# Infini-attention with a mixer MLP, in float32 from pairs: phi read from PSUM, casts and an update on other engines, and a head pipeline of three stages in another order

## The chip, the cores and the metric

The kernel runs on one core of a Trainium2 chip. The metric is the device time of one execution in microseconds (us), median of several runs. The engines are TensorE (PE; its weight loads are shown apart as PEld), VectorE (DVE), ScalarE (ACT), GpSimd (POOL) and SyncE (SP), which here only issues transfers.

## What is computed

2048 tokens of width 1024 pass a pre-norm block: attention with a compressive memory, then an MLP. There are 32 heads of width 32, and 4 segments of 512 tokens.

```python
phi = lambda t: jnp.where(t > 0, t + 1.0, jnp.exp(t))
g = _sigmoid(beta).reshape(1, H, 1, 1)
for s in range(N):
    qs, ks, vs = q[:, :, s], k[:, :, s], v[:, :, s]
    logits = jnp.einsum("bhqd,bhkd->bhqk", qs, ks) * scale + mask
    a_dot = jnp.einsum("bhqk,bhkd->bhqd", _softmax(logits), vs)
    pq = phi(qs)
    num = jnp.einsum("bhld,bhde->bhle", pq, M)
    den = jnp.einsum("bhld,bhd->bhl", pq, z)[..., None] + 1e-6
    outs.append(g * num / den + (1.0 - g) * a_dot)
    pk = phi(ks)
    M = M + jnp.einsum("bhld,bhle->bhde", pk, vs)
    z = z + jnp.einsum("bhld->bhd", pk)
...
h = x + attention(layernorm(x))
h2 = h + (gelu(layernorm(layernorm(h)) @ w1 + b1) @ w2 + b2)
```

The inner softmax is causal within a segment; M and z carry what earlier segments held.

## The kernel before

Float32 products are made of three products of a faster format: each operand is split into a high part (a cast) and a low part (the operand less its high part), and `mm3` (L110) adds high x high, high x low and low x high in PSUM. So every operand costs a cast and a subtraction, and the kernel spreads these over VectorE, ScalarE and GpSimd: for weights `split` (L87) and `load_block` (L193, wh is the high part, wl the low one).

The 2048 tokens go in two halves of two segments each. `attention(half)` (L201) walks over 8 groups g of 4 heads, and for each over its two segments sl. One group in one segment is a *unit* here, so there are 16 units in a half, and a pair of units shares the weights of its group. For a unit, `dense` (L268) makes kps, qps and vps, the transposed projections of 128 x 512, each of 8 steps c of three products (24 steps in all), and `heads` (L482) does the softmax attention of the *previous* unit, one head in each of 4 slots. A slot has 6 steps, written out in `PLAN` (L30), and `interleave` (L509) takes one step of `heads` after each step of `dense`. The order of the program is the order in which each engine gets its instructions, and an engine takes them strictly in that order.

A letter in `PLAN` is one operation of a head, its digit a part of it:

- `q`: scores of one block of queries (TensorE L396 into bank pqk), then VectorE adds the mask and finds the minimum (L397), then ScalarE takes the exponential (L405).
- `n`: VectorE takes reciprocals of the sums (L409), GpSimd scales the rows by them and by 1 - sigmoid(beta) (L412).
- `t`: TensorE transposes the probabilities into bank ppt (L428, group 0, 1 or 2), ScalarE casts them to pth (L430).
- `s`, `S`: VectorE subtracts for ptl (L435).
- `a`: TensorE multiplies with the values (L448, po), ScalarE copies one half of po to ot (L453).
- `o`: VectorE adds the other half (L459); after the fourth head GpSimd adds the memory's part omt (L462), and SP stores it.

Small letters are of the current head or the one before (p1), `S`, `a` and `o` of the one before that (p2): two heads stand in the pipe.

Within `dense`, the projections give more work. kh and qh are casts (ScalarE L277, L291), kl and ql subtractions (VectorE L283, L298); 24 transfers on SP rearrange them per head into ks and qs. phi(k) and phi(q) are min(exp(x), 1) + max(x, 0): ScalarE writes both terms from PSUM (L229, L230), VectorE adds them (L235). pk is transposed (pkn). MZ holds M and z of all groups; its high part mzh is a VectorE cast (L310). `late` (L330) is the rest of a unit and runs in steps during the next unit: vn (values transposed back), the memory's products pm and their division (VectorE L344 to L347 into om), the products pmm of the memory's update (VectorE adds them to M, L362, and the sum of pk to z, L363), and om transposed (pom) and copied (ScalarE L378, omt). The products of pm and pmm are small; they lie in a list, and `one_small` (L249) places one of them ahead of a transposition or a product of `a`.

PSUM has 8 banks: three shared by kps, qps, vps, pkn, vn, pm, pmm and pom, two for pqk, two for ppt, one for po. Temporaries in SBUF come from `tmp` (5 slots) and `tmpr` (6 slots).

The weights of the next group are loaded and split at the end of a pair (`weights`, L490): wh by VectorE (L89), only in the first group's wq and wv by ScalarE (L91); wl by GpSimd (L92). At the start of a half `ln1` (L181) loads x and normalizes it (GpSimd makes the scale factor v, L123 and L124, VectorE or ScalarE applies it); behind attention come the output projection `wo_seg` (L536), the second norm and the MLP, which are not touched.

Of the kernel before, what the change touches and what calls it, by code (L numbers as in the profile page):

```python
# [42 lines left out]
def build(tc, x, wq, wk, wv, wo, beta, w1, b1, w2, b2, out):  # L43
# [157 lines left out]
    def attention(half):  # L201
# [16 lines left out]
        def tmpr(name):  # L218
            return ab.tile([P, 512], F32R, tag="tmpr", name=name, bufs=6)

# [5 lines left out]

        def phi_parts(ps):
            e, r = tmp("e"), tmp("r")
            nc.scalar.activation(e, ps, AF.Exp)  # L229
            nc.scalar.activation(r, ps, AF.Relu)  # L230
            return e, r

        def phi_sum(parts, name, acc=None):
            o = tmp(name)
            nc.vector.scalar_tensor_tensor(o, parts[0], 1.0, parts[1], op0=ALU.min, op1=ALU.add, accum_out=acc)  # L235
            return o
# [11 lines left out]

        def one_small():  # L249
            if small:  # L250
                small.pop(0)()
# [16 lines left out]
        def dense(g, sl, ws, u):  # L268
# [9 lines left out]
            if s < 3:  # L278
                kparts = phi_parts(kps)
            qps = ps_dense("qps")  # L280
            for c in project(ws["q"], sl, "qps", qps):
                if c == 0:
                    nc.vector.tensor_tensor(kl, kps, raw(kh), op=ALU.subtract)  # L283
                    u["ks"] = stack(kh, kl, "ks", (0, 1, 0))
                if c == 2 and s < 3:
                    zc = ab.tile([P, 64], F32, name="zc", bufs=2)[:, 0:1]
                    pk = phi_sum(kparts, "pk", zc)
                next(behind, None)
                yield
            qh, ql = tmpr("qh"), tmpr("ql")  # L290
            nc.scalar.copy(qh, qps)  # L291
            if s > 0:
                qparts = phi_parts(qps)

            vps = ps_dense("vps")
            for c in project(ws["v"], sl, "vps", vps):
                if c == 0:
                    nc.vector.tensor_tensor(ql, qps, raw(qh), op=ALU.subtract)  # L298
                    u["qs"] = stack(qh, ql, "qs", (0, 0, 1))
                if s > 0:  # L300
                    if c == 2:
                        pq = phi_sum(qparts, "pq")
                    if c == 4:
                        while small:
                            one_small()
                        pqh, pql = tmpr("pqh"), tmpr("pql")
                        mzh = ab.tile([P, 256], F32R, name="mzh", bufs=1)[:, 0:132]
                        mzl = ab.tile([P, 256], F32R, name="mzl", bufs=1)[:, 0:132]
                        nc.scalar.copy(pqh, pq)
                        nc.vector.tensor_copy(mzh, MZ[:, g, :])  # L310
                        nc.gpsimd.tensor_tensor(mzl, MZ[:, g, :], raw(mzh), op=ALU.subtract)
                    if c == 5:
                        nc.gpsimd.tensor_tensor(pql, pq, raw(pqh), op=ALU.subtract)
                if c == 1 and s < 3:
                    pkn = ps_dense("pkn")
                    for i in range(4):
                        nc.tensor.transpose(pkn[:, i * P:(i + 1) * P], pk[:, i * P:(i + 1) * P], ident)
# [8 lines left out]
            vs = ab.tile([P, 16, 64], F32R, name="vs", bufs=2)  # L326
            u["vs"] = vs
            omt = u["omt"] = tmp("omt") if s > 0 else None

            def late():  # L330
# [3 lines left out]
                vn3 = vn.rearrange("p (a b) -> p a b", b=DH)  # L334
                nc.scalar.copy(vs[:, :, 0:32], vn3)
                nc.vector.tensor_tensor(vs[:, :, 32:64], vn3, raw(vs[:, :, 0:32]), op=ALU.subtract)
                yield
                if s > 0:
                    om = tmp("om")

                    def memory(i2, ps):
# [3 lines left out]
                        nc.vector.reciprocal(rg, rg)  # L345
                        nc.vector.tensor_tensor(rg, rg, gate[:, 0:1, 4 * g:4 * g + 4].to_broadcast([P, 2, 4]), op=ALU.mult)
                        nc.vector.tensor_tensor(  # L347
# [10 lines left out]
                if s < 3:  # L358
                    def update(pmm):
                        for j in range(4):  # L360
                            b = slice(32 * j, 32 * j + 32)
                            nc.vector.tensor_tensor(MZ[b, g, b], pmm[b, b], MZ[b, g, b], op=ALU.add)  # L362
                        nc.vector.scalar_tensor_tensor(MZ[:, g, 128:132], hsel, zc, MZ[:, g, 128:132], op0=ALU.mult, op1=ALU.add)  # L363

# [5 lines left out]
                while len(small) > total - left:  # L370
                    yield
                yield
                if s > 0:
                    pom = ps_dense("pom")
                    for i in range(4):
                        one_small()
                        nc.tensor.transpose(pom[:, i * P:(i + 1) * P], om[:, i * P:(i + 1) * P], ident)
                    nc.scalar.copy(omt, pom)  # L378
                while small:
# [35 lines left out]
        def ptr(st, n):  # L415
# [21 lines left out]
        def av(st, n):  # L437
# [4 lines left out]
            for jk in (0, 1) if n == 0 else (3, 2):  # L442
                w = 512 - P * jk
                v = u["vs"][:, 4 * jk + j, :]
                for part in ("pth", "ptl"):
                    if (jk, part) != (3, "ptl"):
                        one_small()
                    nc.tensor.matmul(po[:, P * jk:], v, st[part][:, koff[jk]:koff[jk] + w],  # L448
                                     start=(jk, part) == (0, "pth"), stop=(jk, part) == (2, "ptl"))
# [14 lines left out]

        pipe = [None, None]

        def slot(cur):
            p1, p2 = pipe
# [11 lines left out]
            pipe[0], pipe[1] = cur, p1  # L480

# [697 lines left out]
```

## Time and profile before

| | |
|---|---|
| median of 3 runs | 2394.48 us (2393.11 to 2403.72) |
| the profiled execution | 2394.96 us, its span 2393.2 us |
| granted TensorE clock | 0.993 |
| busy: PE, DVE, ACT, POOL | 2308.3, 1628.4, 1212.0, 1065.5 us |
| attention's steady stretches | 60 to 600 us and 960 to 1480 us of the span |

In the views, a row of a stretch gives its start and end, its length, and then for PE, PEld, DVE, ACT and POOL the busy time and in brackets the number of instructions, then the granted clock, the share of the transfer engines and GB/s. A row of the waits names the engine and line that waited, whose result it waited for, the sum, how often, and the longest. A row of groups gives busy time and the mean duration in ns of one, then the idle time ahead of it and what ended that. A row of the timeline gives start and duration, and in square brackets the idle time ahead of it. In the chain a row is start, duration and what the path to the end went through.

### The profile page before, as it was taken

How to read it: one execution, taken by the hardware profiler on the slowest of the kernel's cores; microseconds unless marked ns; L12 is line 12 of the kernel's file. 1: busy time of each engine (PE TensorE's matmuls, PEld its weight loads, DVE VectorE, ACT ScalarE, POOL GpSimd, SP SyncE). 2: the span in 40 equal slices, each digit the busy share in tenths (PEclk: the TensorE clock that was granted, in tenths of full speed). 3: DMA queues.
4: the chain of work that ended last, by engine and by line, in shares of the span. 5: the costliest groups of instructions: out<-in, count | busy, mean ns of one | idle time of the engine just before them, and what ended most of it. 6: DMA issues, size and time to landing. Idle time of an engine off the chain costs nothing.

```text
span 2393.2 us, 35708 instructions
## 1 busy us (share of the span) xinstructions
PE 2308.3 (96%) x11873; PEld 1906.4 (80%) x11873; DVE 1628.4 (68%) x3470; ACT 1212.0 (51%) x2557; POOL 1065.5 (45%) x1011
## 2 busy tenths in 40 slices
PE   6999999999999989999999999999998989999999
PEld 5888888877787878888888877777886878888887
DVE  6777777775475664777777776466565888667763
ACT  4677676775363333677777776254343223232321
POOL 3444444444164442455555544245443554245430
PEclk9999999999999999999999999999999999999999
DMA  5333333333466654433333334366566976476762
GB/s 170 91 89 88 82 84 85 89 105 120 145 207 201 186 151 131 122 85 85 85 86 84 88 95 126 128 211 195 157 187 212 328 258 213 153 251 227 250 222 96
DMA packets 348161, 356.95 MB, mean 149 GB/s; under 512 B 26286, under 2 KB 251594, under 8 KB 347978
## 3 DMA queue, kind: packets, MB, share of 16 engines
q1 hardware_dynamic: 284810, 317.98, 44.3%
q10 hardware_dynamic: 63168, 36.71, 5.2%
q8 instruction: 94, 1.54, 0.3%
q14 instruction: 89, 0.73, 0.1%
HBM read 227.11 MB, written 77.14 MB: 127 GB/s over the span
## 4 chain that ended last, share of the span: by engine, by line
PE 72%; DVE 9%; ACT 6%; DMA 6%; issue 3%; POOL 3%; SPq 1%; ACTq 0%; DVEq 0%; POOLq 0%
PE po L1031 21%; PE bps L656 7%; PE ppt L428 5%; PE dps L656 5%; PE po L448 5%; PE pqk L396 3%; PE kps L111 2%; PE kps L112 2%; PE kps L113 2%; PE vps L111 2%; PE vps L112 2%; PE vps L113 2%; PE pwo L113 2%; PE pwo L111 2%; PE pwo L112 2%
## 5 line engine op out<-in xcount | busy, mean ns | idle before, releaser
L412 POOL TENSOR_SCALAR pr<-pr,nm,gate 128x128 f32<-128x128 f32 (+3 forms) x512 | 322.2, 639 | 409.0 <-DVE nm L409 307.3
L405 ACT ACTIVATE pr<-pr,mx 128x256 f32<-128x256 f32 (+3 forms) x512 | 287.8, 562 | 175.8 <-DVE mx L397 171.3
L397 DVE CUSTOM_DVE_ANT_0 pr<-pqk,mask 128x256 f32<-128x256 f32 (+3 forms) x512 | 243.4, 483 | 38.4 <-PE pqk L396 35.3
L435 DVE TENSOR_TENSOR ptl<-ppt,pth 128x512 fp32r<-128x512 f32 (+1 forms) x384 | 227.2, 597 | 53.5 <-ACT pth L430 51.4
L428 PE MATMUL ppt<-ident,pr 128*128 128x128 f32 x1280 | 222.7, 277 | 1.9 <-DVE ptl L435 1.8
L430 ACT CAST pth<-ppt 128x512 fp32r<-128x512 f32 (+1 forms) x384 | 194.1, 518 | 51.5 <-PE ppt L428 46.5
L92 POOL TENSOR_TENSOR wl<-wr,wh 128x1024 fp32r<-128x1024 f32 x64 | 152.9, 2390 | 103.2 <-ACT wh L91 48.4
L428 PEld LDWEIGHTS ppt<-ident,pr 128*128 128x128 f32 x1280 | 164.0, 140 | 32.1 <-DVE ptl L435 3.6
L1041 DVE TENSOR_TENSOR c<-c,po 128x512 f32<-128x512 f32 x160 | 105.2, 682 | 116.2 <-PE po L1031 115.8
L396 PE MATMUL pqk<-ks,qs 96*128 96x256 f32 (+3 forms) x512 | 162.7, 318 | 1.3 <-DVE mx L397 1.3
L448 PE MATMUL po<-ptl,vs 128*64 128x512 f32 (+3 forms) x512 | 154.2, 311 | 5.8 <-DVE ptl L435 5.6
L448 PE MATMUL po<-pth,vs 128*64 128x512 f32 (+3 forms) x512 | 155.5, 326 | 1.3 <-ACT pth L430 1.1
L888 POOL TENSOR_TENSOR w2r<-w2r 128x512 f32<-128x512 f32 x56 | 90.2, 1622 | 83.9 <-DMA w2r<-in_B_w 70.9
L1031 PE MATMUL po<-w2h,zh 128*128 128x512 f32 x378 | 122.2, 393 | 3.8 <-DVE zh L960 3.3
L409 DVE RECIPROCAL nm<-mx 128x2 f32<-128x2 f32 x256 | 42.2, 165 | 112.6 <-ACT pr L405 112.2
L396 PEld LDWEIGHTS pqk<-ks,qs 96*128 96x128 f32 x512 | 96.0, 188 | 26.4 <-DVE mx L397 6.3
L1031 PE MATMUL po<-w2h,hl 128*128 128x512 f32 x322 | 104.1, 393 | 6.4 <-DVE c L1041 6.4
L111 PE MATMUL vps<-yh,wh 128*128 128x512 f32 x256 | 109.0, 426 | 0.2 <-ACT omt L378 0.2
L111 PE MATMUL kps<-yh,wh 128*128 128x512 f32 x256 | 108.3, 423 | 0.0
L111 PE MATMUL qps<-yh,wh 128*128 128x512 f32 x256 | 107.2, 419 | 0.0
L111 PE MATMUL pwo<-oh,wh 128*128 128x512 f32 x256 | 104.8, 411 | 0.6 <-ACT oh L91 0.6
L113 PE MATMUL pwo<-oh,wl 128*128 128x512 f32 x256 | 101.5, 397 | 0.0
(233 smaller groups left out, 6751.5 us busy)
## 6 DMA issues: line engine op xcount, KB each, us to landing
hr<-h_dram SPq DMA_DIRECT2D x112, 448.0 KB, 5.0
w2r<-in_B_w SPq DMA_DIRECT2D x126, 256.0 KB, 3.9
r<-in_B_w SPq DMA_DIRECT2D x56, 512.0 KB, 4.5
h_dram<-ht ACTq DMA_DIRECT2D x84, 256.0 KB, 3.7
ks<-kh SPq DMA_DIRECT2D x256, 64.0 KB, 2.0
qs<-qh SPq DMA_DIRECT2D x256, 64.0 KB, 2.0
wr<-in_A_wo SPq DMA_DIRECT2D x32, 512.0 KB, 4.4
wx<-in_B_w SPq DMA_DIRECT2D x56, 256.0 KB, 3.6
```

The lines of the kernel that those rows point to most:

```text
L111: nc.tensor.matmul(ps, ah, bh, start=first, stop=False)
L113: nc.tensor.matmul(ps, al, bh, start=False, stop=last)
L396: nc.tensor.matmul(pqk[:, :n], u["qs"][j][:, i * P:(i + 1) * P], u["ks"][j][:, 0:n], start=True, stop=True)
L397: nc.vector.tensor_tensor_reduce(out=st["pr"][:, offs[i]:offs[i] + n], in0=pqk[:, :n], in1=mask[:, 512 - n:512], op0=ALU.add, op1=ALU.min, ...
L405: nc.scalar.activation(pi, pi, AF.Exp, bias=mx[:, i:i + 1], scale=-1.0, accum_out=mx[:, 4 + i:5 + i])
L412: nc.gpsimd.tensor_scalar(pi, pi, nm[:, 4 + k:5 + k], gate[:, 1, 4 * g + j:4 * g + j + 1], op0=ALU.mult, op1=ALU.mult)
L428: nc.tensor.transpose(ppt[:, o:o + P], pr[:, offs[i] + jk * P:offs[i] + (jk + 1) * P], ident)
L430: nc.scalar.copy(pth[:, base:base + w], ppt[:, :w])
L435: nc.vector.tensor_tensor(o, x0, x1, op=ALU.subtract)
L448: nc.tensor.matmul(po[:, P * jk:], v, st[part][:, koff[jk]:koff[jk] + w], start=(jk, part) == (0, "pth"), stop=(jk, part) == (2, "ptl"))
L656: nc.tensor.matmul(ps, x_[:, c, :], y_[:, c, :], start=first and c == 0 and n == 0, stop=last and c == 3 and n == 2, skip_group_check=True)
L1031: nc.tensor.matmul(ps, x_[:, k], y_[k], start=opens and k == 0 and i == 0, stop=closes and k == self.KP - 1 and i == 2, skip_group_check=True)
```

## The change

Line numbers in this section's text are those of the code before.

- phi is computed as max(x, 0) + exp(min(x, 0)). ScalarE writes max(-x, 0) from PSUM and then the exponential of its negative, from SBUF to SBUF; VectorE adds max(x, 0), read from PSUM, to it. It comes at step 1 instead of 2, and the later casts of pq move with it.
- The update of z (L363) is two GpSimd instructions instead of one on VectorE.
- The factor sigmoid(beta) leaves the division (L346) and is applied by ScalarE when it copies pom, as a scale per partition. Its values come in a new tile gate_t, which four small transfers fill ahead of b1 and x.
- mzh is cast by ScalarE, at step 7; pkl is subtracted at step 4.
- All weight casts wh of attention are on ScalarE.
- `tmpr` has 8 slots and ot 2.
- `PLAN` has another order, with the output step `O` of the head three back, so that the pipe holds three.
- `one_small(8)` leaves small products aside between transpositions while 8 or fewer are in the list, two more of the products of `a` take none, and `late` has more empty steps.

```diff
-PLAN = ('q1 S2', 'q0 n0 a0', 'q2 t0 a1', 'q3 n2 s0 o', 't1', 's1 t2')
+PLAN = ('q2 S2', 'q3 O', 'q1 t0 n2', 'q0 a0 s0', 't1 n0', 's1 t2 a1')
...
+    gate_t = const.tile([P, NG], F32, name="gate_t")
+    for j in range(4):
+        nc.sync.dma_start(gate_t[32 * j:32 * j + 32, :],
+                          bass.AP(tensor=beta.tensor, offset=beta.offset + j, ap=[[0, 32], [4, NG]]))
+    nc.scalar.activation(gate_t, gate_t, AF.Exp, scale=-1.0)
+    nc.vector.tensor_scalar(gate_t, gate_t, 1.0, None, op0=ALU.add)
+    nc.vector.reciprocal(gate_t, gate_t)
...
-            return ab.tile([P, 512], F32R, tag="tmpr", name=name, bufs=6)
+            return ab.tile([P, 512], F32R, tag="tmpr", name=name, bufs=8)
...
-        def phi_parts(ps):
-            e, r = tmp("e"), tmp("r")
-            nc.scalar.activation(e, ps, AF.Exp)
-            nc.scalar.activation(r, ps, AF.Relu)
-            return e, r
-
-        def phi_sum(parts, name, acc=None):
+        def below(ps):
+            e = tmp("e")
+            nc.scalar.activation(e, ps, AF.Relu, scale=-1.0)
+            return e
+
+        def phi(ps, e, name, acc=None):
             o = tmp(name)
-            nc.vector.scalar_tensor_tensor(o, parts[0], 1.0, parts[1], op0=ALU.min, op1=ALU.add, accum_out=acc)
+            nc.vector.scalar_tensor_tensor(o, ps, 0.0, e, op0=ALU.max, op1=ALU.add, accum_out=acc)
             return o
...
-        def one_small():
-            if small:
+        def one_small(least=0):
+            if len(small) > least:
                 small.pop(0)()
...
+                    if s < 3:
+                        nc.scalar.activation(ke, ke, AF.Exp, scale=-1.0)
-                if c == 2 and s < 3:
+                if c == 1 and s < 3:
                     zc = ab.tile([P, 64], F32, name="zc", bufs=2)[:, 0:1]
-                    pk = phi_sum(kparts, "pk", zc)
+                    pk = phi(kps, ke, "pk", zc)
...
+                    if c == 1:
+                        pq = phi(qps, qe, "pq")
+                        pqh, pql = tmpr("pqh"), tmpr("pql")
                     if c == 2:
-                        pq = phi_sum(qparts, "pq")
-                    if c == 4:
+                        nc.scalar.copy(pqh, pq)
+                    if c == 3:
+                        nc.gpsimd.tensor_tensor(pql, pq, raw(pqh), op=ALU.subtract)
+                    if c == 7:
                         while small:
                             one_small()
-                        nc.vector.tensor_copy(mzh, MZ[:, g, :])
+                        nc.scalar.copy(mzh, MZ[:, g, :])
...
-                if c == 2 and s < 3:
+                if c == 4 and s < 3:
                     nc.vector.tensor_tensor(pkl, pkn, raw(pkh), op=ALU.subtract)
...
-                        nc.vector.tensor_tensor(rg, rg, gate[:, 0:1, 4 * g:4 * g + 4].to_broadcast([P, 2, 4]), op=ALU.mult)
...
-                        nc.vector.scalar_tensor_tensor(MZ[:, g, 128:132], hsel, zc, MZ[:, g, 128:132], op0=ALU.mult, op1=ALU.add)
+                        zh = ab.tile([P, 4], F32, name="zh", bufs=2)
+                        nc.gpsimd.tensor_scalar(zh, hsel, zc, None, op0=ALU.mult)
+                        nc.gpsimd.tensor_tensor(MZ[:, g, 128:132], MZ[:, g, 128:132], zh, op=ALU.add)
...
-                        one_small()
+                        one_small(8)
                         nc.tensor.transpose(pom[:, i * P:(i + 1) * P], om[:, i * P:(i + 1) * P], ident)
-                    nc.scalar.copy(omt, pom)
+                    nc.scalar.activation(omt, pom, AF.Copy, scale=gate_t[:, g:g + 1])
...
-                    one_small()
+                    one_small(8)
                     o = koff[jk] - base + (i - jk) * P
...
-                    if (jk, part) != (3, "ptl"):
+                    if (jk, part) not in ((0, "pth"), (3, "ptl"), (2, "pth")):
                         one_small()
...
-                    u["ot"] = ab.tile([P, 512], F32, name="ot", bufs=1)
+                    u["ot"] = ab.tile([P, 512], F32, name="ot", bufs=2)
...
-            ops = {"q": (cur, qk), "n": (cur, norm), "N": (p1, norm), "t": (p1, ptr), "s": (p1, sub), "S": (p2, sub),
-                   "a": (p2, av), "o": (p2, av_out)}
+            ops = {"q": (cur, qk), "n": (cur, norm), "t": (p1, ptr), "s": (p1, sub), "S": (p2, sub),
+                   "a": (p2, av), "O": (p3, av_out)}
...
         def tail():
-            yield from slot(None)
-            yield from slot(None)
+            for _ in range(2):
+                yield from slot(None)
+            av_out(pipe[2])
+            yield
...
-                ws[n] = load_block(wp, w, g * P, 3, "vector" if g or n == "k" else "scalar")
+                ws[n] = load_block(wp, w, g * P, 3, "scalar")
```

More of the change, by code (lines that the diff above doesn't have):

```diff
@@ L278, in dense @@
             if s < 3:
-                kparts = phi_parts(kps)
+                ke = below(kps)
             qps = ps_dense("qps")
@@ L292, in dense @@
             if s > 0:
-                qparts = phi_parts(qps)
+                qe = below(qps)
             vps = ps_dense("vps")
@@ L299, in dense @@
                     u["qs"] = stack(qh, ql, "qs", (0, 0, 1))
+                    if s > 0:
+                        nc.scalar.activation(qe, qe, AF.Exp, scale=-1.0)
                 if s > 0:
+                    if c == 1:
+                        pq = phi(qps, qe, "pq")
+                        pqh, pql = tmpr("pqh"), tmpr("pql")
                     if c == 2:
-                        pq = phi_sum(qparts, "pq")
-                    if c == 4:
+                        nc.scalar.copy(pqh, pq)
+                    if c == 3:
+                        nc.gpsimd.tensor_tensor(pql, pq, raw(pqh), op=ALU.subtract)
+                    if c == 7:
                         while small:
                             one_small()
-                        pqh, pql = tmpr("pqh"), tmpr("pql")
                         mzh = ab.tile([P, 256], F32R, name="mzh", bufs=1)[:, 0:132]
                         mzl = ab.tile([P, 256], F32R, name="mzl", bufs=1)[:, 0:132]
-                        nc.scalar.copy(pqh, pq)
-                        nc.vector.tensor_copy(mzh, MZ[:, g, :])
+                        nc.scalar.copy(mzh, MZ[:, g, :])
                         nc.gpsimd.tensor_tensor(mzl, MZ[:, g, :], raw(mzh), op=ALU.subtract)
-                    if c == 5:
-                        nc.gpsimd.tensor_tensor(pql, pq, raw(pqh), op=ALU.subtract)
                 if c == 1 and s < 3:
@@ L463, in av_out @@
                 nc.sync.dma_start(o_dram[u["s"]][u["g"]], ot)
-        pipe = [None, None]
+        pipe = [None, None, None]
         def slot(cur):
-            p1, p2 = pipe
+            p1, p2, p3 = pipe
             def call(st, fn, *args):
@@ L479, in slot @@
                 yield
-            pipe[0], pipe[1] = cur, p1
+            pipe[:] = cur, p1, p2
         def heads(u):
@@ L486, in tail @@
         def tail():
[L487 to L488 removed]
+            for _ in range(2):
+                yield from slot(None)
+            av_out(pipe[2])
+            yield
         def weights(g):
```

6 lines of the change are left out of this document (3 added, 3 removed).

## The prediction

> **What bounds the kernel now.** I read the page's busy times first, then the table by stage, then the waits of TensorE in the two steady stretches of attention.
>
> ```profile
> PE 2308.3 (96%) x11873; PEld 1906.4 (80%) x11873; DVE 1628.4 (68%) x3470; ACT 1212.0 (51%) x2557; POOL 1065.5 (45%) x1011
> ```
>
> TensorE is busy for 96% of the span, the others for at most 68%. The change takes no product and no transposition away, so it can only gain where TensorE stands still or starts its instructions further apart.
>
> ```profile
> 60.00:600.00 540.00, 523.58 (x3124) 437.09 (x3123) 394.71 (x1200) 371.18 (x922) 252.11 (x310) 1.00 0.35 93
> 960.00:1480.00 520.00, 510.79 (x3064) 425.93 (x3065) 398.30 (x1211) 373.86 (x937) 270.42 (x331) 1.00 0.35 93
> ```
>
> In attention TensorE is idle for 540 - 523.58 = 16.4 us and 520 - 510.79 = 9.2 us, 25.6 together: what can be had in the loop. VectorE is 73 to 77% busy, ScalarE 69 to 72%, GpSimd 47 to 52%, and the granted clock is 1.00: no engine but TensorE is near its bound on average, so single late results make the idle time.
>
> ```profile
> PE pmm L261 <- DVE kl L283: 5.9, 7, 0.8
> PE po L448 <- DVE ptl L435: 4.4, 7, 0.7
> PE ppt L428 <- DVE ptl L435: 1.2, 6, 0.4
> ...
> PE pom L377 <- DVE om L347: 2.9, 8, 0.5
> PE pqk L396 <- DVE mx L397: 1.3, 7, 0.2
> PE po L448 <- DVE ptl L435: 1.2, 6, 0.2
> ```
>
> The first three are of the first half, the others of the second. They come once in a pair of units (a unit is one group of heads in one segment). The weight loads show the same stalls longer:
>
> ```profile
> 253.20 0.20 PEld L428 LDWEIGHTS ppt<-ident,pr 128*128 128x128 f32 x2 [0.59 <-DVE ptl L435]
> 256.58 0.13 PEld L448 LDWEIGHTS po<-ptl,vs 128*64 128x64 f32 x1 [1.17 <-DVE ptl L435]
> 281.89 0.19 PEld L261 LDWEIGHTS pmm<-vs,pkh 128*128 128x128 f32 x1 [1.03 <-DVE kl L283]
> ...
> PEld po L448 <- DVE ptl L435: 7.4, 15, 0.6
> PEld pom L377 <- DVE om L347: 4.4, 8, 0.6
> PEld pqk L396 <- DVE mx L397: 4.4, 7, 0.6
> ```
>
> In the first half a pair costs 0.59 + 1.17 + 1.03 = 2.8 us by weight loads and (5.9 + 4.4 + 1.2)/7 = 1.6 by products; I take 2.3, times 7 pairs = 16. In the second it is 16.2 us by weight loads and 5.4 by products over 8 pairs; I take 11. **Stalls of before: 27 us.**
>
> **The change part by part.**
>
> Work taken off VectorE:
>
> ```profile
> L89 DVE CAST wh<-wr x44: 641/687/746, 13.4 to 1366.8; 128x1024 fp32r<-128x1024 f32 x44
> L363 DVE SCALAR_TENSOR_TENSOR MZ<-hsel,zc,MZ x24: 167/790/1364, 36.3 to 1383.8; 128x4 f32<-128x4 f32 x24
> L462 POOL TENSOR_TENSOR ot<-ot,omt x24: 1282/1291/1347, 126.9 to 1481.1; 128x512 f32<-128x512 f32 x24
> L311 POOL TENSOR_TENSOR mzl<-MZ,mzh 128x132 fp32r<-128x132 f32 x8 | 3.8, 472 | 7.5 <-DVE mzh L310 7.5
> ```
>
> That is 44 x 0.69 = 30 us of weight casts and some 24 x 0.79 = 19 of L363: 49 us and a little more, since the gate's product L346 falls away and the small cast L310 goes to ScalarE. All of it is hidden behind TensorE except where it stands ahead of a late subtraction. L363 is worth a look: 128x4 elements take 0.17 us at best and 1.36 at worst, the length of GpSimd's L462 (1.29), so it waits out a GpSimd instruction. Moved to GpSimd it becomes two instructions; L311's 128x132 takes 0.47 there, so at most 0.9 us a time and at least what L363 takes at best, 0.17, hidden at GpSimd's half-empty queue. What waits for it is the next segment's L310, half a unit later or more; without that cover it would cost up to 24 x 0.9 = 22.
>
> ```profile
> L283 DVE TENSOR_TENSOR kl<-kps,kh x9: 691/691/692, 249.7 to 505.0; 128x512 fp32r<-128x512 f32 x9
> L235 DVE SCALAR_TENSOR_TENSOR pk<-e,r x24: 681/683/1041, 35.0 to 1380.3; 128x512 f32<-128x512 f32 x24
> L309 ACT CAST pqh<-pq 128x512 fp32r<-128x512 f32 x8 | 5.3, 664 | 0.1
> L435 DVE TENSOR_TENSOR ptl<-ppt,pth 128x512 fp32r<-128x512 f32 x128 | 88.1, 688 | 26.5 <-ACT pth L430 25.9
> ```
>
> phi's sum now reads PSUM with one operand from SBUF, as L283 does (0.69 against L235's 0.68): plus 0.01. Its Exp now reads SBUF, as L309 does: 0.66 against the 0.58 that L229 shows in the next fence, plus 0.08 on ScalarE, off the path unless queued ahead of a late cast. The banks kps and qps are held until the sum; it is issued a step earlier, so the next taker finds them free: 0. The Trainium skill ("Perfetto Trace Analysis", Optimizing Scalar/DVE Operations) speaks against this edit: it gives a VectorE instruction about 125 ns of access overhead on PSUM and 60 on SBUF. The rows above do not bear that out (0.01, not 0.065); by the rule, an estimate, 15 sums ahead of a late subtraction would make my sum 1 us longer.
>
> **Work put on ScalarE.** All weight casts:
>
> ```profile
> L91 ACT CAST wh<-wr x36: 1038/1054/1072, 21.9 to 1537.6; 128x1024 fp32r<-128x1024 f32 x36
> 248.58 0.58 ACT L229 ACTIVATE e<-kps 128x512 f32<-128x512 f32 x1
> 249.06 0.59 ACT L230 ACTIVATE r<-kps 128x512 f32<-128x512 f32 x1
> 250.88 0.62 ACT L405 ACTIVATE pr<-pr,mx 128x384 f32<-128x384 f32 x1 [1.23 <-DVE mx L397]
> 251.50 0.56 ACT L430 CAST pth<-ppt 128x512 fp32r<-128x512 f32 x1
> 253.78 0.72 ACT L405 ACTIVATE pr<-pr,mx 128x512 f32<-128x512 f32 x1 [1.13 <-DVE mx L397]
> 254.62 0.86 ACT L430 CAST pth<-ppt 128x512 fp32r<-128x512 f32 x2
> ```
>
> 44 casts of 1.05 = 46 us more on an engine that is free for 28%. In an ordinary slot (a unit's 31.9 us, from L283's first and last start over 8 units, by 4 = 8.0) that fits. It clumps in the second slot of a group's second segment. There the instruction order puts wh of k first; it waits until the last k product has read the old block, and behind it stand exp 384, exp 512, kh, Relu, exp 256, Exp and the first cast of pth. From start to start (1.05 overlaps by 0.1): 0.95 + 0.62 + 0.84 + 0.48 + 0.48 + 0.5 + 0.56 + 0.56 = 5.0 us, and VectorE's L435 makes 5.7. The third transposition group wants that bank in the slot's last step, four steps of 8.0/6 = 1.33, less the 0.3 that a product takes: 5.0. **Stall A** is 0.7 (0.4 to 1.2). In the second half pmm waits there for kl: 0.95 + 0.62 + 0.84 + 0.48, then 0.2 and 0.69, ends 3.8 after the last k product, wanted two steps after it, at 2.7: 1.1 (0.9 to 1.35).
>
> **The new order of steps.** The subtraction of the first group and the products on it now lie further apart, so the waits po and pmm of before go. Late next: pmm behind om in the first segment's unit (**B**), priced by pom's longest row above, 0.5 (0 to 0.6), first half only; and the new order's back-to-back 384 and 512 scores behind the cast of q's weights (**C**), between 0 and pqk's 0.6, taken at 0.4. After: (0.7 + 0.5 + 0.4) x 7 + (1.1 + 0.4) x 8 = 23 us, against 27: **-4**. The output step O runs one slot later; its SP transfer passes ks and qs loads that have a slot's time, and the second ot buffer takes the wait away: 0 in the loop, up to 2 us at the two tails. Two more slots of tmpr: 0.
>
> Small products stand between transpositions 15 times a pair instead of 25 times:
>
> ```profile
> 282.06 0.29 PE L428 MATMUL ppt<-ident,pr 128*128 128x128 f32 x1
> 282.11 0.31 PE L261 MATMUL pmm<-vs,pkh 128*128 128x128 f32 x1
> 282.26 0.30 PE L428 MATMUL ppt<-ident,pr 128*128 128x128 f32 x1
> ...
> 41.47 0.44 PE pkn L317 x4
> ```
>
> A pair of them takes 0.20 and a transposition alone 0.11, so a small costs 0.09 there. Beside the wider po products it is nearer its own 0.06 to 0.08; 10 x 0.015 = 0.15 a pair, 15 pairs: **-2.3** (-4.5 to 0).
>
> **Start.**
>
> ```profile
> 0.72 0.39 SPq L64
> 1.16 0.45 SPq L71
> 1.66 4.07 DMA xt<-in_A_x
> ...
> 14.64 2.34 POOL wl L92
> ...
> 22.97 4.76 POOL wl L92 x2
> ...
> 14.70 2.29 DVE L148 SCALAR_TENSOR_TENSOR nb<-mv,v 128x1 f32<-128x1 f32 x1 [0.71 <-POOL v L124]
> ```
>
> Four small loads for gate_t stand ahead of x on SP: 4 x 0.42 = +1.7. The first wl moves behind all four scale factors, so L148 (2.29 us, again as long as GpSimd's wl) is free: -2.3. But wh of k is cast by ScalarE behind the casts of yh and its wl follows only then: 1.05 + 2.39 between the last yh and the first product with wl, less the 2.3, up to 1.1 later. Taken: **-0.5** (-5.4, if the later 4.76 also leaves the chain, to +2.8).
>
> **Sum.** The profiled execution: 2394.96, span 2393.2, with 1.76 us around it, and 0.48 above the median. 2394.96 - 4 - 2.3 - 0.5 = 2388.2; less 0.48, about 2388.
>
> **The rivals.**
>
> 1. **The stalls go instead of moving** (faster). For it: the 49 us leave VectorE, whose results end every wait above, and ScalarE has 28% free. Against: ScalarE's queue in A. If only A stays, 0.7 x 7 + 1.1 x 8 = 14 remain: -13 - 2.8 gives 2379. If nothing stays: 2365. Taken 2378.
> 2. **ScalarE's weight casts pass through** (slower). Each of the 42 casts in the loop stands ahead of an exponential, which holds norm, transposition and pth; if each moves TensorE by 1.05, that is +44, less the 27 and 2.8: 2409. For it: an in-order queue, and a scores' chain that already stops TensorE (pqk behind mx). Against: 2.2 us free on ScalarE in each 8.0 slot. It decides from 40 of 42 casts on; with half of them it is 2387, the forecast.
> 3. **VectorE's freed time buys nothing**, since TensorE is the bound and the same waits come back with other names: 27 stay, only order and start count: 2392.
>
> **How the numbers follow.** Forecast 0.45 (its own range 2381 to 2397), rival 1 0.33, rival 2 0.15, rival 3 0.07. No change means within 0.5%, 12 us, about what a measurement can tell here: 2382.5 to 2406.5. Rival 1 and a little of the forecast give faster 0.36; rival 2 and 0.01 of mishaps at start and tails slower 0.16; the rest 0.48. Range 2371 to 2406: below it lies the part of rival 1 where nothing stays (0.08), above it most of rival 2 (0.1).
>
> **What would show it.** In the waits of TensorE of the changed kernel: po behind ptl and pmm behind kl gone from the first half; ppt behind ptl by 0.4 to 1.2 us once a pair (A), pmm behind kl about 1 us, 8 times, in the second half. L363's successor no longer on VectorE, no VectorE instruction of attention stretched to a GpSimd one. VectorE busy 45 to 65 us less, ScalarE 45 to 55 more. TensorE's idle time in the two stretches near 22. I am wrong if it is under 14 (rival 1), or over 35 with pqk, ppt or po waiting for ScalarE in most slots (rival 2); or if the start moves by over 3 us, seen where L363's first instance (36.3) stands.

## The result, and the profile after

The changed kernel takes 2408.3 us (median of 13 runs, 2403.42 to 2415.17); the kernel before took 2396.74 in the 13 runs beside it (2390.16 to 2403.72). The ratio is 1.0048 (95% interval 1.0035 to 1.0061): slower by 11.6 us, just inside the 0.5% that the prediction called no change, but above the range of 2371 to 2406 and on the other side of the forecast. The profiled execution took 2412.06, its span 2410.2: it lies 3.8 us above its median, and that of before 1.8 below its own, so the two profiles are 17.0 us apart where the medians are 11.6.

Busy times on the page of the changed kernel, then its two steady stretches (columns as before):

```profile
PE 2316.2 (96%) x11873; PEld 1903.3 (79%) x11873; DVE 1587.7 (66%) x3332; ACT 1255.6 (52%) x2626; POOL 1063.9 (44%) x1059
```

```profile
60.00:600.00 540.00, 523.20 (x3127) 436.39 (x3127) 383.31 (x1148) 394.82 (x967) 254.44 (x343) 1.00 0.34 95
960.00:1480.00 520.00, 505.76 (x3043) 420.46 (x3042) 371.69 (x1126) 391.93 (x970) 263.25 (x345) 1.00 0.32 90
```

VectorE is busy 41 us less, ScalarE 44 us more, each a little under what the prediction named (45 to 65 and 45 to 55). TensorE is idle for 16.8 and 14.2 us, 31.0 together, where it was 16.4 and 9.2. The first half kept its idle time, the second grew by 5. Its waits there, first half and then second:

```profile
PE pmm L269 <- DVE om L359: 5.5, 7, 1.0
PE ppt L443 <- DVE nm L424: 5.1, 8, 0.7
PE pqk L411 <- DVE mx L412: 3.0, 8, 0.7
...
PE pqk L411 <- DVE mx L412: 6.9, 8, 0.9
PE pmm L269 <- DVE kl L291: 4.9, 7, 0.7
```

po behind ptl and pom behind om have gone; pmm behind kl has left the first half for the second, pqk behind mx has grown from 1.3 us to 9.9, and ppt behind nm and pmm behind om are new. When a unit's first k product starts, in us of the span (from the timelines), shows where the 17.0 us between the two spans are (unit 2 is the third unit):

| | before | after | later by |
|---|---|---|---|
| unit 0 | 22.10 | 28.97 | 6.9 |
| unit 2 | 77.53 | 87.09 | 9.6 |
| last unit of the first half | 492.13 | 502.08 | 9.9 |
| fourth unit of the second half | 1020.93 | 1032.16 | 11.2 |
| last unit of the second half | 1398.54 | 1415.82 | 17.3 |
| end | 2393.2 | 2410.2 | 17.0 |

9.6 us are lost in the first two units, nothing in the first half's loop (a pair takes 63.69 us before, 63.77 after), and 1.0 us in each of six pairs of the second half (62.94, 63.94). The start's chain after:

```profile
1.17 0.42 SPq L72
...
3.11 0.48 SPq L79
3.64 11.90 DMA xt<-in_A_x
15.57 1.30 DVE st L126 x2
```

L72 issues gate_t's four loads, L79 the load of b1, and L126 is the first work on x. x lands 11.9 us after its issue, where it took 4.07. The transfers of the first 22 us (issues, KB each, median us to landing) of the changed kernel:

```profile
xt<-in_A_x SPq DMA_DIRECT2D x5, 512.0 KB, 11.9
...
gate_t<-in_A_beta SPq DMA_DIRECT2D x4, 1.0 KB, 7.9
```

A load of 1 KB needs 7.9 us, and x, 512 KB, comes behind it. VectorE's own work on gate_t, ahead of its work on x, is not what holds x up, since it ends at 15.06 us and VectorE then waits for x:

```profile
14.86 0.20 DVE L76 RECIPROCAL gate_t<-gate_t 128x8 f32<-128x8 f32 x1
15.57 1.28 DVE L126 BATCH_NORM_STATS2 st<-xt 128x6 f32<-128x512 f32 x2 [0.51 <-DMA xt<-in_A_x]
```

The prediction had paid for the four issues only.

Single executions of one kernel spread by some 12 us, and the granted clock differs from one to the next in the stages behind attention (0.95 before and 0.97 after from 1800 to 1900 us of the profiles). So below, the time of a pair and the start of the first product are read from the profile, beside each ratio with its interval.

### The profile page after: what moved, and what is told of

It reads as the page before. It is cut to its first block, busy times and chain, and to the rows that moved or that the text cites. A ratio compares the mean times of both kernels' runs of the same rounds, so it can differ in the third digit from the quotient of the medians.

```text
span 2410.2 us, 35712 instructions
## 1 busy us (share of the span) xinstructions
PE 2316.2 (96%) x11873; PEld 1903.3 (79%) x11873; DVE 1587.7 (66%) x3332; ACT 1255.6 (52%) x2626; POOL 1063.9 (44%) x1059
## 4 chain that ended last, share of the span: by engine, by line
PE 71%; ACT 9%; DVE 7%; DMA 5%; issue 4%; POOL 2%; SPq 1%; ACTq 0%; DVEq 0%; POOLq 0%
PE po L1048 19%; PE bps L673 8%; PE dps L673 5%; PE po L463 5%; PE ppt L443 4%; PE cps L673 3%; PE pqk L411 2%; PE kps L119 2%; PE kps L120 2%; ACT pr L420 2%; PE kps L121 2%; PE pwo L119 2%; PE vps L119 2%; PE vps L120 2%; PE vps L121 2%
## 5 line engine op out<-in xcount | busy, mean ns | idle before, releaser
L427 POOL TENSOR_SCALAR pr<-pr,nm,gate 128x384 f32<-128x384 f32 (+3 forms) x512 | 307.8, 611 | 406.2 <-DVE nm L424 299.5
L420 ACT ACTIVATE pr<-pr,mx 128x384 f32<-128x384 f32 (+3 forms) x512 | 287.0, 561 | 116.6 <-DVE mx L412 116.1
L412 DVE CUSTOM_DVE_ANT_0 pr<-pqk,mask 128x384 f32<-128x384 f32 (+3 forms) x512 | 235.9, 485 | 23.1 <-PE pqk L411 16.3
L443 PE MATMUL ppt<-ident,pr 128*128 128x128 f32 x1280 | 217.4, 276 | 5.5 <-DVE nm L424 5.1
L443 PEld LDWEIGHTS ppt<-ident,pr 128*128 128x128 f32 x1280 | 159.1, 140 | 34.8 <-issue 10.2
L411 PE MATMUL pqk<-ks,qs 96*128 96x384 f32 (+3 forms) x512 | 165.4, 324 | 10.3 <-DVE mx L412 9.8
L463 PE MATMUL po<-pth,vs 128*64 128x512 f32 (+3 forms) x512 | 149.2, 317 | 0.0
L99 ACT CAST wh<-wr 128x1024 fp32r<-128x1024 f32 x80 | 84.0, 1051 | 77.6 <-PE pwo L120 45.3
L121 PE MATMUL kps<-yh,wl 128*128 128x512 f32 x256 | 101.9, 398 | 2.1 <-POOL wl L100 2.1
```

The source lines that it names most:

```text
L121: nc.tensor.matmul(ps, al, bh, start=False, stop=last)
L411: nc.tensor.matmul(pqk[:, :n], u["qs"][j][:, i * P:(i + 1) * P], u["ks"][j][:, 0:n], start=True, stop=True)
L412: nc.vector.tensor_tensor_reduce(out=st["pr"][:, offs[i]:offs[i] + n], in0=pqk[:, :n], in1=mask[:, 512 - n:512], op0=ALU.add, op1=ALU.min, ...
L420: nc.scalar.activation(pi, pi, AF.Exp, bias=mx[:, i:i + 1], scale=-1.0, accum_out=mx[:, 4 + i:5 + i])
L427: nc.gpsimd.tensor_scalar(pi, pi, nm[:, 4 + k:5 + k], gate[:, 1, 4 * g + j:4 * g + j + 1], op0=ALU.mult, op1=ALU.mult)
L443: nc.tensor.transpose(ppt[:, o:o + P], pr[:, offs[i] + jk * P:offs[i] + (jk + 1) * P], ident)
```

## The experiments

| run | first k product | pair, first half | pair, second half | ratio to before (95%) |
|---|---|---|---|---|
| before | 22.10 | 63.69 | 62.94 | 1 |
| after | 28.97 | 63.77 | 63.94 | 1.0048 (1.0035 to 1.0061) |
| gate_copy | 21.59 | 63.78 | 64.00 | 1.0000 (0.9987 to 1.0014) |
| casts_back | 30.91 | 62.29 | 62.09 | 0.9962 (0.9951 to 0.9973) |
| before_casts | 20.98 | 65.41 | 63.72 | 1.0053 (1.0036 to 1.0069) |
| before_loads | 30.85 | 63.76 | 62.93 | 1.0040 (1.0026 to 1.0053) |
| both | 23.12 | 62.28 | 62.10 | 0.9923 (0.9909 to 0.9937) |
| both_old_order | 22.98 | 63.67 | 62.75 | 1.0022 (1.0009 to 1.0035) |
| both_old_phi | 23.16 | 63.00 | 63.36 | 0.9993 (0.9982 to 1.0003) |
| only_k_back | 23.22 | 62.91 | 63.01 | 0.9964 (0.9949 to 0.9979) |
| late_relu | 23.09 | 61.79 | 62.21 | 0.9926 (0.9909 to 0.9943) |
| both_old_small | 23.15 | 62.81 | 63.06 | 0.9970 (0.9960 to 0.9980) |
| new_order | 22.56 | 64.93 | 63.33 | 1.0052 (1.0032 to 1.0072) |
| loads_in_row | 23.02 | 63.66 | 63.00 | 1.0031 (1.0019 to 1.0042) |
| loads_in_row_2 | 22.58 | 63.57 | 63.00 | 1.0031 (1.0020 to 1.0043) |
| before_loads_2 | 31.08 | 63.53 | 62.99 | 1.0060 (1.0044 to 1.0075) |
| late_loads | 21.03 | 63.79 | 63.97 | 1.0018 (1.0009 to 1.0027) |

The first three columns are in us, each from one profiled execution. A pair is the mean of six, from the first k products of the fourth and the last unit of a half. Two executions of the same start differ by up to 0.5 us in the first column (before and new_order, whose starts have the same code, and loads_in_row and loads_in_row_2).

### The start

**gate_copy**, the changed kernel without the loads:

```diff
-    for j in range(4):
-        nc.sync.dma_start(gate_t[32 * j:32 * j + 32, :], ...)
-    nc.scalar.activation(gate_t, gate_t, AF.Exp, scale=-1.0)
...
+    for j in range(4):
+        nc.vector.tensor_copy(gate_t[32 * j:32 * j + 32, :],
+                              gate[32 * j:32 * j + 32, 0, :].rearrange("p (g j) -> p j g", j=4)[:, j, :])
```

> The changed kernel with gate_t copied on VectorE from the gate tile that is on the chip already, so that the four loads ahead of x are gone. Theory S (the four loads of 4-byte pieces hold the transfer queue, so that x lands 11.9 us after its issue instead of 4.1): x lands near 5.7 us again, the first k product starts at 20 to 23 us instead of 29.0, and the time falls by 7 to 10 us. Rival S0 (they cost only their four issues on SP, 1.9 us, the rest of the late start being the later wl of k): the first k product stays at 26 or later and the time falls by about 2 us. Pairs of units stay at 63.7 us (first half) and 63.95 us (second half) under both.

The first product starts at 21.59 us, the pairs stay, and the ratio falls from 1.0048 to 1.0000, which is 11.5 us, more than the 7 to 10 that were expected. Theory S holds for the start: 7.4 us of this show at the first product.

**before_loads**, the kernel before plus the four loads and three small instructions:

> The kernel before with the four loads of gate_t and its three small instructions added where the change has them, and gate_t not used. Theory S: the first k product starts 7 to 10 us later than 22.1, the whole grows by 7 to 10 us. Rival S0: about 2 us.

The first product comes 8.75 us later, and the ratio is 1.0040: the loads alone make a late start. **loads_in_row** asks whether the small pieces cost it or four more loads of any kind:

```diff
-                          bass.AP(tensor=beta.tensor, offset=beta.offset + j, ap=[[0, 32], [4, NG]]))
+                          bass.AP(tensor=beta.tensor, offset=beta.offset + NG * j, ap=[[0, 32], [1, NG]]))
```

> The kernel of the run named before_loads, with the four loads reading eight neighbouring values per partition (32 bytes in a row) instead of eight values four apart; as many bytes, partitions and issues; gate_t is not used. Theory P (the 256 pieces of 4 bytes of each load hold the queue): the loads land in 2 to 4 us instead of 7.9, x lands near its old time plus the 1.9 us of issues, the first k product starts at 23 to 25 us instead of 30.85. Rival Q (four more loads of any kind hold it): the first k product at 29 us or later.

The transfers of its first 22 us:

```profile
xt<-in_A_x SPq DMA_DIRECT2D x7, 512.0 KB, 4.6
...
gate_t<-in_A_beta SPq DMA_DIRECT2D x4, 1.0 KB, 2.6
```

With the same bytes, issues and partitions, but 32 pieces of 32 bytes a load instead of 256 of 4, a load lands in 2.6 us instead of 8.0 and the first product comes 0.9 us late instead of 8.75. (The profiles of before_loads and loads_in_row count 1342 and 478 packets under 512 bytes in these 22 us.) So the division into pieces held the queue, whether by their number or their size, and not the four loads as such. The whole does not follow, though: 1.0031 is 7 us. Both kernels were run again, on one chip.

> The kernel of loads_in_row again. It cost 7 us while its first k product came only 0.9 us later. If that was scatter of the long stages behind attention (granted clock there 0.93 against 0.95): ratio 0.9995 to 1.0015. If the loads cost time elsewhere too, by a way that does not show at the start: ratio 1.002 to 1.004 again.

> The kernel of before_loads again, on one chip with loads_in_row_2. If the start is all that the pieces cost: 7 to 9 us above loads_in_row_2. If what was measured there was mostly something else: within 4 us of it.

The ratios are 1.0031 again and 1.0060. The pieces cost 2408.52 - 2402.14 = 6.4 us, between the two cases expected, where the first product shows 31.08 - 22.58 = 8.5. Some 6 us come with the loads in a way that the start does not show. In the profile of loads_in_row_2 the loop's pairs are as before, and the stretch from the last unit of the first half to the first of the second takes 445.6 us against 441.07; why, no run shows. **late_loads** keeps the changed kernel's loads of 4 bytes but issues them behind the first unit:

> The changed kernel with the same four loads of 4-byte pieces issued behind the first unit's projections instead of ahead of x, and their three small instructions behind the second unit. If the place ahead of x is what costs: the first k product at 21 to 23 us, and the time 8 to 12 us below the changed kernel's, as in gate_copy (ratio to before 0.998 to 1.001). If the loads or the tile cost time elsewhere too: ratio 1.002 or more.

The first product starts at 21.03 us, the stretch between the halves takes 440.64, and the ratio of 1.0018 lies between its two cases. The place ahead of x makes most of the cost, 0.0030 or 7 us of 11.5; the cause of the remainder stays open.

### The weight casts on ScalarE

**casts_back** and **before_casts** undo and do this part alone, by one word:

```diff
-                ws[n] = load_block(wp, w, g * P, 3, "scalar")
+                ws[n] = load_block(wp, w, g * P, 3, "vector" if g or n == "k" else "scalar")
```

> The changed kernel with the weight casts back where they were (VectorE, except q and v of the first group). Theory C (the weight casts ahead of exponentials and of kh and ot on ScalarE's queue make the waits pqk behind mx, pmm behind kl and pmm behind om): a pair falls from 63.7 to 62.0-62.7 us in the first half and from 63.95 to 62.0-62.8 us in the second, the whole by 14 to 25 us. Rival O (the new order of steps makes these waits, the output addition standing ahead of the next minimum on VectorE): pairs change by less than 0.4 us, the whole by less than 5 us; VectorE's casts of 0.69 then stand in the same places.

> The kernel before with all weight casts on ScalarE and nothing else changed. Theory C: pairs grow from 63.8 and 62.95 us by 0.7 to 2 us, the whole by 10 to 30 us. Rival O: pairs stay within 0.4 us, the whole within 5 us.

Theory C holds in both. In the changed kernel the casts cost 63.77 - 62.29 = 1.5 us and 63.94 - 62.09 = 1.85 us a pair, about 10 + 15 = 25 us over 7 and 8 pairs (by the ratios, 1.0048 against 0.9962, 21 us); in the kernel before they cost 1.7 and 0.8 a pair. The timeline of the second half of the changed kernel shows how, first where the cast of k's weights falls (start, duration):

```profile
1233.58 1.05 ACT L99 CAST wh<-wr 128x1024 fp32r<-128x1024 f32 x1 [0.76 <-PE kps L120]
1234.54 0.61 ACT L420 ACTIVATE pr<-pr,mx 128x384 f32<-128x384 f32 x1
1235.15 0.71 ACT L420 ACTIVATE pr<-pr,mx 128x512 f32<-128x512 f32 x1
1235.97 0.59 ACT L285 CAST kh<-kps 128x512 fp32r<-128x512 f32 x1
1236.59 0.69 DVE L291 TENSOR_TENSOR kl<-kps,kh 128x512 fp32r<-128x512 f32 x1
1237.34 0.33 PE L269 MATMUL pmm<-vs,pkh 128*128 128x128 f32 x1 [0.70 <-DVE kl L291]
```

The cast of k's weights goes ahead of two exponentials and of kh, so kl ends at 1237.3 and TensorE's pmm has stood for 0.70 us behind it: the prediction's chain, link by link. And half a unit later, where the cast of q's weights falls:

```profile
1247.39 1.06 ACT L99 CAST wh<-wr 128x1024 fp32r<-128x1024 f32 x1
1248.33 0.65 ACT L311 ACTIVATE e<-e 128x512 f32<-128x512 f32 x1
1248.86 0.86 ACT L445 CAST pth<-ppt 128x512 fp32r<-128x512 f32 x2
1249.74 0.62 ACT L317 CAST pqh<-pq 128x512 fp32r<-128x512 f32 x1
1250.39 0.58 ACT L468 COPY ot<-po 32x512 f32<-32x512 f32 x1
1251.00 0.68 DVE L474 TENSOR_TENSOR ot<-po,ot 32x512 f32<-32x512 f32 x1 [0.36 <-ACT ot L468]
1251.61 0.53 DVE L412 CUSTOM_DVE_ANT_0 pr<-pqk,mask 128x384 f32<-128x384 f32 x1
1252.20 0.39 PE L411 MATMUL pqk<-ks,qs 96*128 96x256 f32 x1 [0.94 <-DVE mx L412]
```

Here the cast of q's weights delays Exp, pth, pqh and the copy of ot. The output step O stands ahead of the next minimum on VectorE, so the minimum waits for ot too, and the third block of scores, which has two banks to go to, waits 0.94 us until the minimum has read one. **only_k_back** separates the two (gate_t copied, `"vector" if n == "k" else "scalar"`):

> The changed kernel with gate_t copied from the gate tile and only the k weights' casts back on VectorE; q and v stay on ScalarE. The prediction's stall A hangs on k's cast, its stall C on q's. Theory (each cast makes its own wait): pmm behind kl leaves the second half and ppt behind nm the first, pqk behind mx stays; pairs 62.9 to 63.3 us and 62.9 to 63.3 us. Rival (ScalarE's load as a whole, not the place): all waits shrink by a third, pairs near 63.3 and 63.35 us with every wait still there.

Against gate_copy (63.78 and 64.00) k's cast makes 0.87 and 0.99 us of a pair, q's and v's together the other 0.63 and 0.91. ppt behind nm in the first half and pmm behind kl in the second fall to 0.7 us each, in two cases and in one, while pqk behind mx stays at 6.9: each cast makes its own wait.

### Both undone

> The changed kernel with both undone: gate_t copied from the gate tile, weight casts where they were before. Theory (the two costs are separate and add up): the first k product starts at 21.5 to 22.5 us, pairs take 62.3 us (first half) and 62.1 us (second), and the whole is 14 to 19 us below the kernel before, ratio 0.992 to 0.994. Rival (the start comes back by another way, since before too the first product waited for a wl of GpSimd, or the gain is lost at the tails): at most 9 us below.

The costs add up: 2381.16 us, 0.9923, 17 us below the kernel before by the medians and 18 by the ratio. This version beats both kernels. Its first product starts at 23.12 us, 0.6 later than the theory had it. What is left of its waits, first half and then second:

```profile
PE pmm L266 <- DVE om L356: 5.3, 7, 0.8
...
PE pqk L408 <- DVE mx L409: 3.6, 8, 0.7
```

The other edits gain 63.69 - 62.28 = 1.4 and 62.94 - 62.10 = 0.85 us a pair. Four runs take them apart, three of them from this kernel.

**both_old_phi**: phi's two terms from PSUM by ScalarE and their sum from SBUF, as before, at the new step:

```diff
-            nc.scalar.activation(e, ps, AF.Relu, scale=-1.0)
-            return e
+            nc.scalar.activation(e, ps, AF.Exp)
+            nc.scalar.activation(r, ps, AF.Relu)
+            return e, r
...
-            nc.vector.scalar_tensor_tensor(o, ps, 0.0, e, op0=ALU.max, op1=ALU.add, accum_out=acc)
+            nc.vector.scalar_tensor_tensor(o, e[0], 1.0, e[1], op0=ALU.min, op1=ALU.add, accum_out=acc)
```

> The kernel of the run named both, with phi from both its terms as before (ScalarE makes both from PSUM, VectorE adds them from SBUF) at the changed kernel's step. Prediction's price (0.01 us for reading PSUM, 0.08 for an Exp that reads SBUF): pairs within 0.3 us of 62.3 and 62.1. Rival (the Exp's place in the queue, one step later than before and ahead of the first pth cast, is a cost): pairs 0.3 to 1.0 us shorter.

Neither came: pairs are longer, by 0.7 and 1.3 us, so the new form is a gain. The rows of phi(q)'s sum, of both_old_phi and then of both (minimum, median and maximum in ns):

```profile
L241 DVE SCALAR_TENSOR_TENSOR pq<-e,r x24: 679/1408/1807, 69.8 to 1425.1; 128x512 f32<-128x512 f32 x24
```

```profile
L240 DVE SCALAR_TENSOR_TENSOR pq<-qps,e x24: 666/681/692, 68.5 to 1410.6; 128x512 f32<-128x512 f32 x24
```

And at one instance in both_old_phi:

```profile
1233.19 1.41 DVE L241 SCALAR_TENSOR_TENSOR pq<-e,r 128x512 f32<-128x512 f32 x1
...
1231.65 2.39 POOL L97 TENSOR_TENSOR wl<-wr,wh 128x1024 fp32r<-128x1024 f32 x1
```

With both operands in SBUF the sum waits out GpSimd's wl, until 1234.04; with one in PSUM none of 24 is stretched. It stands ahead of ptl, ot and the next minimum on VectorE, and in the second half TensorE's wait for that minimum is 11.1 us where both has 3.6:

```profile
PE pqk L405 <- DVE mx L406: 11.1, 9, 1.8
```

The old form has another cost that no run separates from this one: ql, ahead of the sum on VectorE, also waits for ScalarE's second term (0.81 us idle at this instance). On the stretched sum, the Trainium skill ("SBUF — State Buffer", Who interferes with whom) has this rule: a VectorE instruction with two SBUF inputs contends with a GpSimd one that reads SBUF, one with a single SBUF input doesn't. The trace agrees with both sides of it.

**both_old_order** has the old PLAN and a pipe of two. **new_order** is the kernel before with only the new PLAN, the pipe of three and the second ot.

> The kernel of the run named both, with the order of steps and the pipe of two of the kernel before; all else of the change stays (phi, update of z, gate in the copy, small products). Theory N (what is gained beside the casts is the new order's): pairs 63.2 to 63.8 us and 62.7 to 63.1 us, with po behind ptl back among the waits. Rival V (it comes from work that left VectorE): pairs stay at 62.3 and 62.1 us within 0.3.

> The kernel before with only the new order of steps, the pipe of three and the second ot buffer. Theory N (the order makes the gain by itself): pairs near 62.3 us in both halves. Rival NP (the order pays only with phi from PSUM, whose terms leave ScalarE's queue sooner; without it exp 384 and exp 512 are late): pairs at 63.0 and 63.3 us or more, with pqk behind mx as in the run named both_old_phi.

Without the new order the gain is gone in the first half (63.67) and mostly gone in the second (62.75), but by other waits than expected: pmm behind phi(k)'s sum (7.8 us) and pkn behind ql (3.2) in the first half, qps behind om (5.0) and pkn behind omt (3.9) in the second. Alone, the new order loses 1.2 and 0.4 us a pair. Waits of new_order, first half and then second:

```profile
PE ppt L428 <- DVE nm L409: 6.0, 10, 0.8
PE qps L111 <- ACT omt L378: 4.5, 7, 0.6
PE pqk L396 <- DVE mx L397: 3.7, 8, 2.6
...
PE qps L111 <- DVE kl L283: 4.9, 6, 0.8
```

qps waits until omt's copy or kl has read the bank that it takes. So the order does not make the gain by itself: it pays only with other edits of the change, and they with it. Which of them it needs (the places of phi and pkl, the empty steps of `late`, the two slots of tmpr) no run shows.

**both_old_small** places the small products as before.

> The kernel of the run named both, with the small products placed as before (one ahead of each transposition while there are any, and ahead of more products of the attention values). The prediction took the new placing for a gain of 0.15 us a pair. By that: pairs 62.4 and 62.25 us. Rival: their place also moves the wait for om and kl, and pairs grow by over 0.5 us.

The old placing costs 0.53 and 0.96 us a pair, where the prediction had 0.15. In the first half the waits of TensorE are no longer with the old placing (pmm and ppt 4.2 + 1.7 = 5.9 us, against 5.3 + 0.7 = 6.0), so there TensorE does not stand still longer but starts its instructions further apart; why by so much is open.

**late_relu**: phi(k)'s Relu behind kl, from the kernel both:

```diff
-            if s < 3:
-                ke = below(kps)
...
                     if s < 3:
+                        ke = below(kps)
                         nc.scalar.activation(ke, ke, AF.Exp, scale=-1.0)
```

> The kernel of the run named both, with phi(k)'s Relu issued after kl's subtraction instead of ahead of it. What is left there is one wait per pair in the first half, pmm behind om by 0.8 us: om stands behind kl on VectorE, and kl waits until ScalarE has done the Relu too. Theory: kl and om come about 0.5 us earlier, a pair of the first half falls from 62.28 to 61.8-62.0 us, the whole by 2 to 4 us. Rival (pk comes later by as much and its transposition or the bank of kps waits instead): pairs of the first half at 62.2 us or more.

Pairs of the first half fall from 62.28 to 61.79, and the wait behind om from 5.3 us to 2.4:

```profile
PE pmm L266 <- DVE om L355: 2.4, 7, 0.3
```

So om did wait behind kl, and kl behind a Relu that it doesn't need (in the changed kernel kl waits for that Relu, L238, in 22 cases, 14.6 us in all). In the whole (0.9926) this kernel cannot be told from both.

## Why the prediction was wrong

The forecast was a gain of 6.8 us: 4 from stalls, 2.3 from small products, 0.5 from the start. Two steps failed, by about as much each. The four loads, priced at +1.7, cost 11.5 us by the ratios (1.0048 against 1.0000 in gate_copy). All the rest, priced at -8.5, came to nothing: gate_copy takes as long as the kernel before, give or take 3 us.

- **What bounds the kernel** held: TensorE does the same 11873 products and transpositions, and what moved is its idle time and the distance of its starts.
- **The start.** "4 x 0.42 = +1.7" priced each load by its issue on SP, and the bound of +2.8 with it. Landing was what counted: 7.9 us for 1 KB, with x behind it. Measured: 6.9 us at the first product, 9.6 by the third unit; a start later by over 3 us was one of the prediction's own signs of being wrong. The profile of before had a small load's landing (bb, 16 KB, 3.6 us), which the sum did not use, but no load in pieces of 4 bytes. The other start terms (L148 free, wl later) come with the casts and were taken at -2.2 us together. L148 did get free (0.16 us instead of 2.29), and three pairs of runs that differ by the casts alone give -1.1 (before, before_casts), -1.5 (both, gate_copy) and -1.9 (casts_back, after).
- **The price of the stalls of before** (27 us) is where the loop's sum went wrong. It is a mean of two measures, the waits of the weight loads and those of the products, while the stalls after (23 us) were worked out for the products alone. By the products' rows alone, before had 11.5 + 5.4 = 16.9 us, so that the same terms would have forecast a loss of 6 and not a gain of 4, all of it in the second half. The rows after give 25.4 us, and the second half is where the pairs grew, by 1.0 us each. That this comes so near is partly luck, since other terms were off too.
- **The stalls after** were in the right places and somewhat mis-sized. A was right: the cast of k's weights makes 0.87 and 0.99 us a pair, predicted 0.7 and 1.1. (In the first half the profile puts that wait of ppt down to nm; nm is no operand of that ppt, and ptl, whose bank it takes, ends beside it.) C was 0.63 and 0.91 with v's cast in it, predicted 0.4: the chain through ot and O to the next minimum was not seen. B is the wait behind om, 5.5 us in 7 pairs, 0.8 each for 0.5; kl, issued ahead of om on VectorE, makes it, and late_relu takes more than half of it away.
- **The small products** were mis-sized by three to six times (0.15 against 0.53 and 0.96 a pair).
- **phi from PSUM** was priced at +0.01, from medians at the old place. L235's maximum of 1041 ns stood in the quoted row, and L363's stretch beside it was explained by GpSimd, but the two were not joined: at the new step GpSimd's wl runs beside the sum, and the old form would cost 0.7 and 1.3 us a pair. The dearer PSUM access that the prediction weighed by the Trainium skill ("Perfetto Trace Analysis", Optimizing Scalar/DVE Operations) does not show: the sum of phi(q) from PSUM has the median of the one from SBUF before, 681 against 679 ns.
- **The rivals.** Rival 2's mechanism, casts that stand in ScalarE's queue ahead of what the path needs, took the loop's gain, at about half its price: 42 casts cost 25 us by the pairs in the changed kernel, 0.6 each, and less by the ratios, where 1.05 was the price. Rival 1's 2378 is near the 2381 of both, but by luck: it counted on 49 us leaving VectorE, and in both the 30 us of weight casts are on VectorE again. No rival named the start.

So the change is three things: edits that gain some 18 us, casts that take away about as much (0.9923 in both, 1.0000 in gate_copy), and loads that add the 11.5, of which the cause is shown for the late start and open for the rest. The sum by pairs (25 us for the casts) is larger than the 18 that these ratios show; the stages behind attention differ by several us from one execution to the next.

## What to carry to other kernels

Price a small load by its landing and by what is queued behind it, not by its issue: here four loads of 1 KB in pieces of 4 bytes held up one of 512 KB by 8 us. An engine with 28% of its time free can still be the wrong place for a 1 us cast: look at which instructions stand behind it in order, at the slot where it is issued. Where an instruction moves, read its maximum and not its median, and which other engine made it long, for the new place can make the maximum the rule. And take the stalls before and after by one and the same measure.

## What the runs showed of the hardware

A copy from PSUM on ScalarE with a scale per partition from a tile takes longer than without. Rows of the changed kernel and of the kernel before:

```profile
L393 ACT ACTIVATE omt<-pom,gate_t x24: 687/688/692, 104.0 to 1471.0; 128x512 f32<-128x512 f32 x24
```

```profile
L378 ACT COPY omt<-pom x24: 566/586/591, 95.3 to 1445.2; 128x512 f32<-128x512 f32 x24
```

That is 0.1 us, which the prediction had not priced. The scale from a tile is what differs: ScalarE's Relu from PSUM with a constant scale, L238 of the changed kernel, takes 578 to 596 ns (medians). The two GpSimd instructions that replace L363 take 0.29 and 0.20 us, inside the bounds given.
